# A multi-head attention block on one core: new written-out lists for every engine, and score products with 128-column query weights

## The chip, the core and the metric

The kernel runs on one core of a Trainium2 chip. Five engines each follow a list of their own: TensorE (PE, matrix products; its weight loads are shown as PEld), VectorE (DVE), ScalarE (ACT), GpSimd (POOL) and SyncE (SP), which here only issues DMAs. They wait for one another through semaphores. The metric is the device time of one execution in microseconds (us); lower is better.

## What is computed

```
B, Sq, D = 8, 112, 640          H, Sk, Dh = 32, 512, 192        (all bf16)
q = (x @ wq).reshape(B, Sq, H, Dh).transpose(0, 2, 1, 3)
scores = einsum("bhqd,bhkd->bhqk", q, k_cache) * Dh ** -0.5
p = softmax(scores)
o = einsum("bhqk,bhkd->bhqd", p, v_cache)
out = o.transpose(0, 2, 1, 3).reshape(B, Sq, H * Dh) @ wo
```

The key and value caches are 50 MB each; x, wq, wo and the result are small beside them.

## The kernel before

The 32 heads are taken in four **rounds** of eight. A round goes over the eight batches, and each batch of a round is two **steps** of four heads: 64 steps, numbered n = 0 to 63. Two half-rounds (batches 0 to 3 and 4 to 7) make a **group** g = 0 to 7, which has its own projections and its own output products, each 448 columns wide (4 batches of 112 rows).

What an entry of a list means, with the helper that builds it:

- `XT`, `evX`: x is transposed on TensorE and copied to `xT_sb` (7 pieces).
- `Q(g, lp, c)`, `evQ` (q_fill): five products of 128x448 make a third of the queries of one head pair; ACT copies them to `qr`. 96 entries.
- `KT(i, p)`, `evK` (k_transposes): the keys of the first seven batches are loaded as they are (`KN`), transposed on TensorE and copied to `kt`. From batch 7 on a DMA transposes them on the way (`K`).
- `qc(n)`: DVE copies parts of `qr` to `qh`, moved by 64 partitions, as the 192 dimensions of a head are 128 + 64.
- `Sm(n, j)`, `St(n, ...)` (scores): the score products. Queries are the weights, keys the moving operand. Sm holds eight products per step over all 128 rows of the array; St holds eight over 64 rows each, which run two at a time on the two halves. They always use PSUM banks 0 to 3.
- `smax`, `exp`, `rc`, `norm` (softmax): DVE copies a head's scores to `s_sb` (three buffers) with the row minimum of the negated scores, ACT takes the exponential with its sum, DVE takes the reciprocal and scales. Four heads per step.
- `PT(n)`, `evPT` (transposes): 32 small transposes turn the probabilities; ACT and DVE copy half each to `pT_sb`. For steps 57 to 61 a DMA does it instead (`TD`).
- `PVt`, `PVm`, `evPV` (values): the products with the values, 16 that use half of the array's columns and 16 full ones; ACT copies the result to `oT_sb`.
- `O(g, m, part)`, `oacc`: twelve products per block m of the output, in two halves, added up in `accT`. `O6`, `OL`, `OF`, `oout` and `OUT` do the last batches, the final transposes and the stores.

So TensorE has three shapes on its array: full (XT, Q, Sm, PVm, O, OF), row halves (KT, St, PT) and column halves (PVt).

The order is not left to a planner: `ORDER_PE`, `ORDER_ACT`, `ORDER_DVE` and `ORDER_SP` are lists in the code, and each engine runs its own strictly in order. An entry waits for those named as its dependencies, and for the copies that free its PSUM bank; the bank stands in the entry of ORDER_PE, and `fill` adds the wait. The loads go out on SP's one queue in ORDER_SP's order: a load waits at the head of the queue until its buffer is free (four buffers for keys, three for values, one for wo, four separate pieces for wq). `exp` of step n also waits for PT or TD of step n - 2, whose probabilities lie in the same buffer.

The lines of the profile: L546 XT, L561 KT, L590 Q, L635 and L637 Sm, L648 and L650 St, L706 PT, L739 PVt, L750 PVm, L772 O; L572 evK, L595 evQ, L612 and L613 qc, L663 smax, L668 exp, L672 norm, L680 rc, L719 evPT, L760 evPV, L787 oacc; L139 K, L150 V, L162 X, L171 KN, L183 WQ, L193 WO, L690 TD. L578 are idle products before any data has come.

## Time and profile before

| | |
|---|---|
| time, three runs | 443.73, 445.71 and 450.0 us; median 445.71 |
| span of the profiled execution | 444.4 us (no time around the span is given) |
| PE busy | 425.1 us, 96% of the span, 6805 products |
| weight loads busy | 304.5 us, 69% |
| DVE busy | 363.2 us, 82% |
| ACT busy | 344.4 us, 78% |
| SP | 100 DMAs, 122 MB moved, 275 GB/s |
| granted TensorE clock, mean | 0.996 |

Busy times on PE overlap: a product begins before the one ahead has drained. What a product costs when they follow one another is the distance of two starts, which the timeline gives. In a row of groups, the number after the busy time is the mean duration in ns of one instruction, and behind the bar stands the idle time of the engine just before such instructions with what ended it. In a merged row of the timeline, "x5" says how many instructions it holds, and its length runs from the first start to the last end.

### The profile page before, as it was taken

The numbers are of one execution on the slowest core, as the hardware profiler recorded it, in microseconds if no ns is written. First come the engines' busy times: TensorE is split into PE (matmuls) and PEld (weight loads), VectorE is DVE, ScalarE is ACT, GpSimd is POOL, SyncE is SP. The second block draws the span as 40 slices with busy tenths as digits, with TensorE's granted clock in tenths as the row PEclk, the third lists the DMA queues.
The fourth block names the chain that finished last, engine by engine and source line by source line (L and its number), as shares of the span: only waits on it lengthen the run. The fifth ranks groups of instructions, "written<-read, shape, count | busy, mean of one in ns | idle before, by whom it ended". The sixth has DMA issues, their size and how long they took to land.

```text
span 444.4 us, 16108 instructions
## 1 busy us (share of the span) xinstructions
PE 425.1 (96%) x6805; PEld 304.5 (69%) x6805; DVE 363.2 (82%) x1165; ACT 344.4 (78%) x770; POOL 0.7 (0%) x6
## 2 busy tenths in 40 slices
PE   6998989889999999999899999999999999899995
PEld 4666666666677667777677766767667766676895
DVE  1579999879699889888989798889799888969871
ACT  3699999887678687978869688788778758965773
POOL 0000000000000000000000000000000000000000
PEclk9999999999999999999999999999999999989999
DMA  8999999998999999999999999999999999999952
GB/s 278 373 337 323 347 299 285 226 342 276 232 289 317 215 270 270 365 247 288 238 223 324 301 236 267 360 370 234 234 266 313 256 267 371 234 173 242 237 176 80
DMA packets 222184, 122.02 MB, mean 275 GB/s; under 512 B 164640, under 2 KB 222112, under 8 KB 222112
## 3 DMA queue, kind: packets, MB, share of 16 engines
q1 hardware_dynamic: 222112, 120.99, 106.6%
q8 instruction: 54, 0.88, 0.8%
q14 instruction: 18, 0.15, 0.1%
HBM read 78.22 MB, written 1.15 MB: 179 GB/s over the span
## 4 chain that ended last, share of the span: by engine, by line
PE 84%; DVE 5%; ACT 5%; DMA 4%; issue 2%; SPq 0%; ACTq 0%
PE ps L772 19%; PE ps L590 18%; PE ps L750 12%; PE ps L648 7%; PE ps L739 7%; PE ps L635 6%; PE ps L637 6%; PE ps L706 5%; DVE s_sb L663 3%; DMA wo_sb<-in_k_cache_dram 2%; PE ps L561 2%; ACT p_sb L668 2%; DMA wq_sb<-in_wq_dram 2%; ACT qr L595 1%; DVE p_sb L672 1%
## 5 line engine op out<-in xcount | busy, mean ns | idle before, releaser
L668 ACT ACTIVATE p_sb<-s_sb,nmx 112x512 bf16<-112x512 f32 x256 | 182.8, 717 | 31.6 <-DVE s_sb L663 26.8
L663 DVE TENSOR_SCALAR_CACHE_REDUCE s_sb<-ps 112x512 f32<-112x512 f32 x256 | 169.4, 684 | 29.6 <-PE ps L650 20.8
L590 PE MATMUL ps<-xT_sb,wq_sb 128*128 128x448 bf16 x480 | 102.0, 353 | 3.3 <-DMA wq_sb<-in_wq_dram 2.3
L772 PE MATMUL ps<-oT_sb,wo_sb 128*128 128x448 bf16 (+1 forms) x480 | 93.3, 341 | 0.1
L672 DVE TENSOR_SCALAR p_sb<-p_sb,rinv 112x512 bf16<-112x512 bf16 x256 | 81.3, 347 | 1.5
L590 PEld LDWEIGHTS ps<-xT_sb,wq_sb 128*128 128x128 bf16 x480 | 42.9, 98 | 41.5 <-DMA wq_sb<-in_wq_dram 2.9
L772 PEld LDWEIGHTS ps<-oT_sb,wo_sb 128*128 128x128 bf16 x480 | 44.3, 98 | 35.0 <-DVE pT_sb L719 0.5
L760 ACT ACTIVATE oT_sb<-ps 128x672 bf16<-128x672 f32 x64 | 46.3, 726 | 25.8 <-PE ps L750 25.4
L595 ACT ACTIVATE qr<-ps 128x448 bf16<-128x448 f32 x96 | 49.6, 539 | 12.7 <-PE ps L590 12.1
L750 PE MATMUL ps<-pT_sb,vt 128*128 128x112 bf16 x944 | 55.8, 215 | 2.0 <-issue 2.0
L719 ACT ACTIVATE pT_sb<-ps 128x768 bf16<-128x768 bf16 x59 | 47.0, 801 | 12.8 <-PE ps L706 12.8
L750 PEld LDWEIGHTS ps<-pT_sb,vt 128*128 128x128 bf16 x944 | 48.1, 99 | 6.3 <-issue 2.1
L668 ACT ACTIVATION_READ_ACCUMULATOR p_sb<-s_sb,nmx 112x1 f32 x256 | 49.5, 193 | 0.0
L719 DVE COPY pT_sb<-ps 128x1024 bf16<-128x1024 bf16 x59 | 40.3, 683 | 3.4 <-PE ps L706 2.6
L706 PE MATMUL ps<-ident,p_sb 64*128 64x64 bf16 (+1 forms) x1888 | 37.3, 185 | 1.2 <-issue 0.6
L706 PEld LDWEIGHTS ps<-ident,p_sb 64*128 64x128 bf16 (+1 forms) x1888 | 33.3, 94 | 5.8 <-DVE p_sb L672 2.0
L635 PE MATMUL ps<-kt,qr 128*112 128x256 bf16 x128 | 36.0, 282 | 0.9 <-ACT oT_sb L760 0.4
L637 PE MATMUL ps<-kt,qh 128*112 128x256 bf16 x128 | 35.2, 275 | 1.1 <-issue 1.1
L635 PE MATMUL ps<-kt,qh 128*112 128x256 bf16 x128 | 35.1, 274 | 0.0
L637 PE MATMUL ps<-kt,qr 128*112 128x256 bf16 x128 | 35.0, 274 | 0.0
L650 PE MATMUL ps<-kt,qh 64*112 64x256 bf16 x128 | 34.1, 291 | 0.1
L648 PE MATMUL ps<-kt,qr 64*112 64x256 bf16 x128 | 34.0, 291 | 0.0
(62 smaller groups left out, 478.6 us busy)
## 6 DMA issues: line engine op xcount, KB each, us to landing
vt<-in_v_cache_dram SPq DMA_DIRECT2D x32, 1536.0 KB, 9.0
wo_sb<-in_wo_dram SPq DMA_DIRECT2D x4, 1920.0 KB, 12.7
wq_sb<-in_wq_dram SPq DMA_DIRECT2D x14, 480.0 KB, 5.7
wo_sb<-in_k_cache_dram SPq DMA_DIRECT2D x3, 1536.0 KB, 9.3
accT<-in_k_cache_dram SPq DMA_DIRECT2D x3, 1536.0 KB, 12.7
vt<-in_k_cache_dram SPq DMA_DIRECT2D x2, 768.0 KB, 10.0
out_dram<-xT_sb SPq DMA_DIRECT2D x8, 140.0 KB, 3.2
wq_sb<-in_wq_dram SPq DMA_DIRECT2D x1, 960.0 KB, 10.6
```

Source lines behind the costliest of these rows:

```text
L590: mm = e.matmul(ps[:, bank, 0:SG], wq_sb[:, dc, c0:c0 + 128], xT_sb[:, dc, bh * SG:(bh + 1) * SG], start=(dc == 0), stop=(dc == DC - 1))
L595: return e.activation(qr[:, q_slot(g, lp), c, :], ps[:, bank, 0:SG], ACTF.Copy)
L635: e.matmul(ps[0:SQ, 2 * j, hs], ev, ktb[:, :, 0, cs(i)], start=(h == 0), stop=False, skip_group_check=True)
L637: mm = e.matmul(ps[0:SQ, 2 * j + 1, hs], od, ktb[:, :, 2, cs(i)], start=(h == 0), stop=False, skip_group_check=True)
L648: m1 = e.matmul(ps[0:SQ, 2 * j, hs], ev, ktb[0:64, :, 1, cs(i)], start=False, stop=True, skip_group_check=True)
L663: return e.tensor_scalar(s_sb[:, a, :].rearrange("p (e c) -> p e c", e=2), ps[0:SQ, 2 * j:2 * j + 2, h * 256:(h + 1) * 256], -scale, None, ...
L668: return e.activation(p_sb[:, k, :], s_sb[:, a, :], ACTF.Exp, bias=nmx[:, k:k + 1], scale=-1.0, accum_out=rsum[:, k:k + 1])
L672: return e.tensor_scalar(p_sb[:, k, :], p_sb[:, k, :], rinv[:, k:k + 1], None, op0=ALU.mult)
L706: ends.append(e.transpose(psb[:, bank + t, i * w:(i + 1) * w], p_sb[lo:hi, (4 * n + k) % 8, q * 128:(q + 1) * 128], ident[lo:hi, lo:hi]))
L719: return e.activation(dst, src, ACTF.Copy) if j == 0 else e.tensor_copy(dst, src)
L750: mm = e.matmul(ps[:, b0 + j, 2 * h * SQ:(2 * h + 1) * SQ], vtb[:, h0 + 2 * j + h, d0:d0 + 128], pT(j, h, q), start=(q == 0), stop=(q == 3))
L772: mm = e.matmul(ps[:, bank_of["O", g, m, 0], 0:nc_], wo_sb[:, k, m * 128:(m + 1) * 128], oT_sb[:, g % 2, k, 0:nc_], start=(k == 0), stop=( ...
```

## The change

Three things change; the products keep their number, their rows and their moving operands.

1. **All lists are new**: the order of TensorE, ACT, DVE and of the loads, and the PSUM bank of each tile, which now stands in a list `BANKS` of its own. Which of ACT and DVE copies a tile now follows from the list that holds the copy: ACT has 22 key copies (25 before) and five of x (four), DVE 34 and two. Bank waits are found from the list (`tiles`, `holder`), and each of them names all copies of the bank. St comes as two entries per step instead of four, so other work may stand between Sm and St.
2. **Score products read 128 query columns** as their weights, where they read 112. The buffers `qr` and `qh` become flat, `qr` with 16 columns of padding behind each head pair (`QP = 3 * SG + 16`); the 16 extra columns are the neighbour's queries or zeros and make score rows 112 to 127, which nothing reads. DVE clears the padding at the start, and TensorE waits for that.
3. Some **dependencies are written out**: the reciprocal waits for the normalisations two steps back, a copy of PV or of the transposed probabilities names all three entries of the step.

The core of the diff:

```diff
-        qr = sb("qr", [128, QS, 3, SG], BF16)
-        qh = sb("qh", [128, 2, 2, 4, SQ], BF16)
+        qr = sb("qr", [128, QS * QP], BF16)
+        qh = sb("qh", [128, 2 * 2 * 4 * SQ + 16], BF16)
...
+        def q_at(n, j, c, lo, hi):
+            r, b, qd = place(n)
+            c0 = (q_slot(group(n), 2 * qd) + j) * QP + c * SG + b % (B // 2) * SQ
+            return qr[lo:hi, c0:c0 + 128]
+        def h_at(n, j, k, lo, hi):
+            c0 = ((n % 2 * 2 + j) * 4 + k) * SQ
+            return qh[lo:hi, c0:c0 + 128]
...
-                        e.matmul(ps[0:SQ, 2 * j, hs], ev, ktb[:, :, 0, cs(i)], start=(h == 0), stop=False,
+                return e.matmul(ps[:, 2 * j + odd, hs], q, ktb[lo:hi, :, blk, cs(2 * j + h)],
+                                start=first, stop=last, skip_group_check=True)
...
-                add("DVE", ("rc", n, j), [("exp", n, 2 * j), ("exp", n, 2 * j + 1)], rc)
+                add("DVE", ("rc", n, j), [("exp", n, 2 * j), ("exp", n, 2 * j + 1),
+                                          ("norm", n - 2, 2 * j), ("norm", n - 2, 2 * j + 1)], rc)
...
         ORDER_SP = [
-            ("X", 0), ("X", 1), ("WQ", 0, 1, 1), ("WQ", 0, 0, 1), ("KN", 0, 0, 4), ("X", 2), ("WQ", 0, 2, 2),
+            ('WQ', 0, 1, 1), ('X', 1), ('X', 0), ('WQ', 0, 0, 1), ('X', 2), ('WQ', 0, 2, 2), ('KN', 0, 0, 4),
...
-            ("V", 23), ("V", 25), ("K", 28), ("K", 27), ("K", 29), ("V", 27), ("V", 26), ("WO", 3), ("V", 28),
-            ("K", 30), ("K", 31), ("TD", 57), ("TD", 58), ("V", 29), ("TD", 59), ("V", 30), ("TD", 60), ("TD", 61),
+            ('V', 26), ('K', 29), ('K', 30), ('V', 28), ('V', 27), ('V', 29), ('K', 31), ('TD', 57), ('TD', 58), ('WO', 3),
+            ('TD', 59), ('V', 30), ('TD', 60), ('TD', 61), ('V', 31), ('OUT', 1), ('OUT', 0), ('OUT', 2), ('OUT', 5),
...
+        for op in ORDER_PE:
+            for bank, evacs in tiles(op):
+                P.ops[op]["banks"] = P.ops[op]["banks"] + holder.get(bank, [])
+                holder[bank] = evacs
...
+            e.memset(qr[:].rearrange("p (l w) -> p l w", w=QP)[:, :, 3 * SG:QP], 0.0)
+            e.memset(qh[0:64, 0:16 * SQ].rearrange("p (j k s) -> p j k s", j=4, k=4)[:, :, 0, :], 0.0)
+            e.memset(qh[64:128, 0:16 * SQ].rearrange("p (j k s) -> p j k s", j=4, k=4)[:, :, 3, :], 0.0)
+            e.memset(qh[:, 16 * SQ:], 0.0).then_inc(zINIT, 1)
```

TensorE's new list, near round 3's first output products (ORDER_PE), and DVE's at step 58 (ORDER_DVE):

```
PE:  ... ('St', 59, 1), ('O', 5, 2, 1), ('PVt', 55), ('PVm', 55, 0), ('PVm', 55, 1), ('Sm', 60, 0), ('Sm', 60, 1),
     ('St', 60, 0), ('St', 60, 1), ('PVt', 58), ('PVt', 56), ('PVm', 56, 0), ('PVm', 56, 1), ('PVm', 58, 0), ('PVm', 58, 1),
     ('Sm', 61, 0), ('Sm', 61, 1), ('St', 61, 0), ('St', 61, 1), ('PVt', 57), ('PVm', 57, 0), ('PVm', 57, 1), ('O', 6, 1, 0) ...
DVE: ... ('rc', 58, 0), ('rc', 58, 1), ('norm', 58, 1), ('norm', 58, 3), ('norm', 58, 2), ('oacc', 5, 4), ('norm', 58, 0) ...
```

The code has two more forms that the change does not use: pairs of projections over half the rows (`QPAIRS`, empty) and score products over half the rows alone (`ROWS`, empty).

## The prediction

> **What bounds the kernel now.** First the page: the span, the busy shares, the chain that ended last.

> ```profile
> span 444.4 us, 16108 instructions
> PE 425.1 (96%) x6805; PEld 304.5 (69%) x6805; DVE 363.2 (82%) x1165; ACT 344.4 (78%) x770; POOL 0.7 (0%) x6
> PE 84%; DVE 5%; ACT 5%; DMA 4%; issue 2%; SPq 0%; ACTq 0%
> ```

> TensorE carries 84% of the chain, so the time is its list plus its gaps. The windows say where the gaps are; the columns are us of busy time and instructions of PE, weight loads, DVE, ACT and POOL, then clock, DMA share and GB/s.

> ```profile
> 0.00:40.00 40.00, 36.63 (x530) 23.52 (x530) 21.68 (x63) 27.74 (x57) 0.70 (x6) 1.00 0.95 322
> 40.00:80.00 40.00, 36.04 (x817) 26.93 (x816) 37.76 (x120) 38.12 (x84) 0.00 (x0) 1.00 1.08 315
> 80.00:93.30 13.30, 11.68 (x247) 8.22 (x245) 11.09 (x37) 11.33 (x25) 0.00 (x0) 1.00 1.11 269
> 120.00:160.00 40.00, 40.00 (x586) 28.07 (x585) 35.58 (x113) 30.86 (x71) 0.00 (x0) 1.00 1.19 271
> 280.00:320.00 40.00, 39.95 (x599) 27.52 (x600) 33.52 (x111) 32.94 (x75) 0.00 (x0) 1.00 1.14 302
> 360.00:400.00 40.00, 37.44 (x580) 27.20 (x579) 33.44 (x111) 29.51 (x69) 0.00 (x0) 0.96 1.08 267
> ```

> There are two stages. From 40 to 80 us DVE (37.76 of 40) and ACT (38.12) are full and TensorE waits for them. From 120 us on TensorE is full (40.00) and they have room. A busy PE is not one at its peak, so I take what an instruction costs from the starts of neighbours:

> ```profile
> 153.41 0.27 PE L635 MATMUL ps<-kt,qh 128*112 128x256 bf16 x1
> 153.42 0.13 PEld L637 LDWEIGHTS ps<-kt,qr 128*112 128x112 bf16 x1
> 153.52 0.27 PE L637 MATMUL ps<-kt,qr 128*112 128x256 bf16 x1
> 153.73 0.31 PE L648 MATMUL ps<-kt,qr 64*112 64x256 bf16 x1
> 154.30 0.98 PE L739 MATMUL ps<-pT_sb,vt 128*64 128x112 bf16 x32
> 155.21 1.75 PE L750 MATMUL ps<-pT_sb,vt 128*128 128x112 bf16 x32
> 156.79 1.11 PE L590 MATMUL ps<-xT_sb,wq_sb 128*128 128x448 bf16 x5
> ...
> 378.32 0.27 PE L637 MATMUL ps<-kt,qr 128*112 128x256 bf16 x1
> 378.52 0.31 PE L648 MATMUL ps<-kt,qr 64*112 64x256 bf16 x1
> 378.90 0.27 PE L650 MATMUL ps<-kt,qr 64*112 64x256 bf16 x1
> 379.10 0.74 PE L590 MATMUL ps<-xT_sb,wq_sb 128*128 128x448 bf16 x3
> ```

> A main score product starts 0.11 us after the one before (153.41, 153.52). Where the shape on the array changes, it is 0.20 to 0.21 (153.52 to 153.73), so a change of shape costs 0.095. A projection product takes (1.11 - 0.35)/4 = 0.19, a value product 1.75/32 = 0.05, a narrow one 0.98/32 = 0.03.

> **The change, part by part.** *The 128 columns.* The weight loads, grouped by shape:

> ```profile
> L635 PEld LDWEIGHTS ps<-kt,qr 128*112 128x112 bf16 x128 | 16.7, 130 | 8.6 <-DVE s_sb L663 3.1 <-issue 0.8 <-ACT oT_sb L760 0.5
> L648 PEld LDWEIGHTS ps<-kt,qr 64*112 64x112 bf16 x128 | 16.0, 125 | 11.4 <-issue 11.4
> L590 PEld LDWEIGHTS ps<-xT_sb,wq_sb 128*128 128x128 bf16 x480 | 42.9, 98 | 41.5 <-DMA wq_sb<-in_wq_dram 2.9 <-ACT kt L572 1.0 <-issue 0.6
> ```

> A load of 112 columns takes 125 to 130 ns, one of 128 takes 98. Eight groups of 128 make 1024 score loads; 1024 x 32 ns is 33 us of busy time that goes. But each load lies beside the product before it (load at 153.42, its product at 153.52, products 0.11 apart without a gap), so that cover hides it. The change of shape does not show it either: 378.32 to 378.52 waits for a load of 112 columns and 378.90 to 379.10 for one of 128, and both are 0.20. What can still be open is the first load after a wait, at most one per step and 64 x 32 ns = 2 us. Bounds: 0 to 2 us gained, and below that 33 us if all were exposed, which the rows exclude. I take 0. [...]

> *TensorE's list.* It holds the same 736 entries. Counted in the two lists, changes of shape between neighbours fall from 254 to 246: 8 x 0.095 = 0.8 us off.

> *The first loads.* The query weights' first piece now goes ahead of the two pieces of x.

> ```profile
> 0.74 0.97 SPq L162 DMA_DIRECT2D kt<-in_x_dram  x2
> 4.41 1.28 PE L546 MATMUL ps<-ident,kt 128*128 128x128 bf16 x20
> 7.66 1.12 PE L590 MATMUL ps<-xT_sb,wq_sb 128*128 128x448 bf16 x5 [1.97 <-DMA wq_sb<-in_wq_dram]
> 9.08 0.74 PE L590 MATMUL ps<-xT_sb,wq_sb 128*128 128x448 bf16 x3 [0.29 <-DMA wq_sb<-in_wq_dram]
> 19.09 0.69 DVE L663 TENSOR_SCALAR_CACHE_REDUCE s_sb<-ps 112x512 f32<-112x512 f32 x1 [1.66 <-PE ps L650]
> ```

> The same bytes are there at about 7.6 us, but the transposes of x (1.28 us in all) and their copies, hidden under the wait until now, then stand behind them: the first projection starts near 9.0 instead of 7.66, 1.4 later; the wait at 9.08 (0.3) goes. Net +1.0 (0.5 to 2.3). The extra memsets at the start lie before 4.41 and cost nothing.

> *The first ten steps.* Here DVE and ACT set the pace. Up to the last normalisation of step 9 DVE's list has 33 key evacuations instead of 30, one more row minimum (smax), one query copy (qc) and one copy of x fewer. From the rows

> ```profile
> L663 DVE TENSOR_SCALAR_CACHE_REDUCE s_sb<-ps 112x512 f32<-112x512 f32 x256 | 169.4, 684 | 29.6 <-PE ps L650 20.8 <-PE ps L648 4.2 <-ACT p_sb L668 3.5
> L572 DVE COPY kt<-ps 128x768 bf16<-128x768 bf16 x31 | 16.5, 551 | 10.5 <-PE ps L561 10.5
> L612 DVE COPY qh<-qr 64x672 bf16<-64x672 bf16 x64 | 21.1, 329 | 4.0 <-PE ps L650 1.2 <-ACT qr L595 0.9
> 92.41 0.88 DVE L672 TENSOR_SCALAR p_sb<-p_sb,rinv 112x512 bf16<-112x512 bf16 x3
> 95.68 0.63 PE L706 MATMUL ps<-ident,p_sb 64*128 64x64 bf16 x32
> ```

> that is 3 x 0.55 + 0.68 - 0.66 - 0.5, or 1.2 us more of busy time and, as neighbours overlap by some 0.08, about 0.9 more of pace. In the trace that normalisation ends at 92.41 + 0.88 = 93.3 and step 9's transposes start at 95.68. TensorE's list ahead of them, by the spacings above (34 projection entries of five x 0.19, 11 steps of scores at 1.30, 28 key entries at about 0.31, nine transposes at 0.44, eight value steps at 1.22, x 2.0, 57 changes of shape at 0.095), is 76.3 us, so TensorE had stood 19.4 us by then. In the new list it is 72.1 (29 projections, 12 steps of scores, 27 key entries, 52 changes of shape): scores come earlier, projections later. With the same DVE gaps step 9's transposes follow at 93.3 + 0.9 = 94.2, and TensorE has stood 22.1: 2.7 worse. DVE's gaps are 40 - 21.68 = 18.3 before 40 us, and 2.2 + 2.2 from there to 93.3; by busy time these 4.4, by pace some 7, would vanish at best: 87.3, and TensorE has stood 15.2: 4.2 better. TensorE's larger lead argues for fewer DVE gaps; I take the middle, -1, the later start included.

> *The middle.* From 120 us TensorE was full. The work between a step's last score product and its own transposes, which hides the softmax chain, falls at the median over the steps from 12.2 to 11.7 us; its least value up to step 56 falls from 9.4 to 8.8. The room behind a transpose before its banks are wanted again falls from 3.4 to 2.9, behind a value product from 1.9 to 1.5. That costs 0 if the chains still fit, 5 us if each of some ten tight places loses half a microsecond. I take +1. Against it stand waits for nothing in the list:

> ```profile
> PE ps L750 <- issue: 2.0, 1, 2.0
> PE ps L561 <- issue: 2.0, 2, 1.1
> PE ps L637 <- issue: 1.1, 1, 1.1
> ```

> These 5 us may recur elsewhere or go; I leave them in.

> *The loads.* The same hundred DMAs stand in one queue in another order; a key transpose holds the queue some 6.8 us when others follow. The output weights of round 3 now stand behind the transposing DMAs of steps 57 and 58.

> ```profile
> 386.93 6.83 SPq L139 DMA_TRANSPOSE kt<-in_k_cache_dram  x1
> 398.29 4.36 SPq L690 DMA_TRANSPOSE wq_sb<-p_sb  x2
> wo_sb<-in_wo_dram SPq DMA_DIRECT2D x4, 1920.0 KB, 12.7
> DMA to landing us min/median/max: 7.1/12.0/14.7
> ```

> They may start once O(5,2,1) is done and step 58's normalisation, which now waits behind oacc(5,4) on DVE, has let its DMA be issued. From O(5,2,1) to the first use, O(6,1,0), the new list has 8.2 us of TensorE's work (four narrow entries, eight value entries, two steps of scores, eight changes of shape); the old one had 22.9. The load takes 12.7 at the median, beside other loads; 7.1, the least of a 1536 KB load into the same tile, scaled to 1920 KB, is an estimated 8.9. About 0.7 goes to the issue of step 58's DMA. Bounds: 8.9 + 0.7 - 8.2 = 1.4 to 14.7 + 0.7 - 8.2 = 7.2. No other load is released beside it, so near the lower end: +2. Behind TensorE's wait stand the score products of steps 62 and 63, the last ones. The same transposing DMA feeds step 58's values, 10.6 us of list behind its scores; that fits within half a microsecond and is taken as 0. The reciprocal's new wait names normalisations of DVE's own list two steps back, long done: 0. The other loads keep the lead that they had or more than a landing, but KN(4): 8.1 us instead of 20.5, bounds 0 to 2, taken as 0.

> **The sum.** 444.4 - 0.8 - 1 + 1 + 2 = 445.6 in the profiled execution's own terms (its span; no time around it is given). The three runs have median 445.71, 1.3 above that span; so 446.9, rounded to **446.5**.

> **The rivals.** *DVE becomes the bound for longer, slower.* In steps 9 to 12 DVE's list lies within some 3 us of TensorE's in the new order, 8 to 11 us before. An item that comes late on DVE's strict list then stops TensorE at once. DVE's list up to step 11's last normalisation is 79.5 us by pace, TensorE's ahead of that step's transposes 82.3. If DVE has gaps of 30 us by then (93.3 less 68.1 us of list is 25 at step 9 in this trace), TensorE stands 79.5 + 30 - 82.3 = 27 us, not some 20: +7. With the sum's +1 and +2 it is 444.4 - 0.8 + 7 + 1 + 2 = 453.6, or 455 as a median, +2.1%; from those 30 us it decides. For it: the full window of 40 to 80. Against it: DVE waited mostly for TensorE (20.8 us behind L650 in the row above), which now brings scores earlier. 18%.

> *The late output weights alone.* 7.2 instead of 2 gives 452: +1.4%. 12%.

> *The early gaps go.* -4.2 instead of -1, the 5 us of issue waits gone, +1 for the loads: 444.4 - 0.8 - 4.2 - 5 + 1 = 435.4, about 436.7, -2.0%. Against it: start and evacuations leave no more. 18%, half of it beyond 2%.

> *The loads set the score products' pace.* If each of the 512 main products had to wait for its load, 512 x 32 ns = 16 us would go: 430. The rows speak against it: 0.11 apart with loads of 0.13 beside. 3%. [...]

> **How the numbers follow.** The forecast has 49%, the rivals 18, 12, 18 and 3. Faster by over 2% (about what a measurement of this kernel can tell from no change): 9 + 3 = 12%. Slower: the first rival's 18%. Within: 49 + 12 + 9 = 70%. The range leaves out the fall by the loads and most of the slow tail: 437 to 456.

> **What would show it.** Score loads at 98 ns with products still 0.11 apart: the columns are worth nothing. First projection near 9.0. Step 9's transposes between 87 and 94 us. TensorE full from 120 us. A wait of TensorE for wo_sb of 1 to 7 us after 395 us. The prediction is wrong if products stand closer than 0.11, if TensorE still has gaps past 120 us for DVE or ACT, or if step 9 comes after 97.

## The result, and the profile after

The changed kernel takes 461.04 us at the median of four runs (459.41 to 465.59), the kernel before 445.25 beside it: 1.0352 times as long, 95% interval 1.0265 to 1.0438. That is slower, and outside the range. The profiled execution is the longest of the four, 465.59, so its parts add up to some 4.5 us more than the median.

First the page of the changed kernel: span, busy shares, the chain that ended last.

```profile
span 463.8 us, 16105 instructions
PE 432.8 (93%) x6805; PEld 291.7 (63%) x6805; DVE 365.4 (79%) x1171; ACT 343.3 (74%) x768; POOL 0.7 (0%) x6
PE 67%; DVE 13%; DMA 11%; issue 4%; ACT 3%; SPq 0%; DVEq 0%; ACTq 0%
```

TensorE's share of the chain has fallen from 84% to 67%; DVE and DMA have taken it. So the list of TensorE no longer sets the time alone. The windows say where (columns: busy time of PE, weight loads, DVE, ACT, POOL, then clock, DMA share, GB/s). First three of the kernel before that are not shown above, then the changed kernel:

```profile
93.30:120.00 26.70, 25.46 (x405) 17.84 (x403) 20.05 (x63) 18.51 (x43) 0.00 (x0) 1.00 1.01 268
320.00:360.00 40.00, 39.77 (x592) 27.84 (x590) 35.53 (x114) 31.50 (x71) 0.00 (x0) 1.00 1.17 266
400.00:444.00 44.00, 39.55 (x630) 33.05 (x627) 29.16 (x97) 26.80 (x58) 0.00 (x0) 1.00 0.73 185
```

```profile
40.00:80.00 40.00, 32.87 (x724) 23.18 (x725) 34.63 (x110) 32.98 (x72) 0.00 (x0) 0.98 1.00 271
80.00:93.30 13.30, 12.45 (x263) 8.32 (x262) 10.49 (x33) 10.68 (x22) 0.00 (x0) 0.93 1.06 375
93.30:120.00 26.70, 22.89 (x406) 15.82 (x404) 20.92 (x69) 20.75 (x48) 0.00 (x0) 0.94 0.93 204
120.00:160.00 40.00, 39.66 (x618) 26.24 (x610) 34.65 (x114) 31.21 (x71) 0.00 (x0) 1.00 1.17 250
320.00:360.00 40.00, 36.31 (x468) 22.72 (x466) 28.35 (x94) 26.89 (x63) 0.00 (x0) 0.91 1.15 291
400.00:440.00 40.00, 37.19 (x437) 24.41 (x438) 32.51 (x110) 23.08 (x58) 0.00 (x0) 0.96 0.99 211
```

Three places lose: 40 to 120 us, 320 to 360, 400 to 440. In each the granted clock is below 1 too (0.93 to 0.98, then 0.91, then 0.96). What TensorE waited for (sum, times, longest, in us):

```profile
PE ps L911 <- DMA wo_sb<-in_wo_dram: 4.8, 2, 2.7
PE ps L877 <- issue: 3.4, 2, 3.2
PE ps L744 <- issue: 3.4, 1, 3.4
PE ps L688 <- DMA wq_sb<-in_wq_dram: 1.5, 2, 0.9
PE ps L877 <- DMA vt<-in_v_cache_dram: 1.2, 2, 0.7
PE ps L744 <- DMA kt<-in_k_cache_dram: 0.9, 1, 0.9
```

Before, no load of this table held TensorE after 50 us. Now four kinds do, and the waits for nothing ("issue") reach 3.4 us each. The timeline shows what stands behind such a gap (L688 Q, L744 scores, L845 PT, L877 and L889 the values, L911 O):

```profile
8.96 2.61 PE L688 MATMUL ps<-xT_sb,wq_sb 128*128 128x448 bf16 x10 [0.68 <-DVE xT_sb L134]
...
78.48 0.37 PE L744 MATMUL ps<-kt,qh 64*128 64x256 bf16 x1 [3.40 <-issue]
...
78.81 3.52 PE L688 MATMUL ps<-xT_sb,wq_sb 128*128 128x448 bf16 x10
...
97.51 0.64 PE L845 MATMUL ps<-ident,p_sb 64*128 64x64 bf16 x31
...
109.16 0.68 PE L877 MATMUL ps<-pT_sb,vt 128*64 128x112 bf16 x9 [3.18 <-issue]
...
335.36 2.40 PE L911 MATMUL ps<-oT_sb,wo_sb 128*128 128x448 bf16 x6 [2.69 <-DMA wo_sb<-in_wo_dram]
...
422.17 5.06 PE L911 MATMUL ps<-oT_sb,wo_sb 128*128 128x448 bf16 x17 [2.10 <-DMA wo_sb<-in_wo_dram]
```

Ten projection products behind the gap at 78.48 take 3.52 us, 0.35 apart on average instead of 0.19. The granted clock of this trace is 0.50 from 78.4 us on for 3.4 us, and likewise at the other three gaps of over 2 us: from 109.1 for 3.4, from 334.4 for 6.8, from 423.1 for 3.4. That is 17.1 us at half the clock, which the table below prices at 7.9, beside 11.4 us for the four gaps themselves.

And the load queue (SPq; the middle number is how long the loads held it until the last was issued):

```profile
251.18 29.43 SPq L142 DMA_TRANSPOSE kt<-in_k_cache_dram  x3
...
293.50 27.21 SPq L142 DMA_TRANSPOSE kt<-in_k_cache_dram  x3
320.77 0.57 SPq L153 DMA_DIRECT2D vt<-in_v_cache_dram  x1
321.39 0.58 SPq L196 DMA_DIRECT2D wo_sb<-in_wo_dram  x1
```

The output weights of round 2 (L196) could have gone at 314.2, when the last output product of round 1 was done. They went at 321.39, behind three key transposes, landed at 335.2, and TensorE stood.

To compare runs I add up TensorE's standing time from the starts of neighbouring products: what a start lies later than the usual spacing of its kind (0.19 for a projection, 0.11 for a score product and so on, and 0.095 for a change of shape), from 0.06 us on, by the releaser that the trace names. Without a releaser I count up to 0.195 us too late as the half clock, more as a wait for nothing. In us, each from one profiled execution:

| | span | DVE | ACT | loads | nothing | half clock |
|---|---|---|---|---|---|---|
| before | 444.4 | 3.3 | 4.4 | 4.1 | 6.7 | 1.6 |
| changed | 463.8 | 10.5 | 2.2 | 9.3 | 11.0 | 7.9 |
| e1 old lists | 443.4 | 4.3 | 4.2 | 3.5 | 7.5 | 3.1 |
| e2 112 columns | 458.4 | 11.1 | 2.0 | 5.6 | 11.0 | 3.4 |
| e5 without K7, K8 | 453.4 | 9.6 | 2.7 | 6.7 | 7.1 | 5.7 |
| e9 new lists, few loads | 444.1 | 11.2 | 2.8 | 1.7 | 5.0 | 2.8 |
| e10 old lists, few loads | 436.5 | 4.9 | 4.1 | 5.3 | 0.5 | 0.9 |
| e12 other order at 300 us | 460.5 | 10.5 | 2.1 | 7.6 | 13.3 | 4.1 |
| e14 as e9, short minima | 436.7 | 2.9 | 4.0 | 2.4 | 4.7 | 2.3 |
| e15 as e10, short minima | 432.2 | 1.1 | 5.1 | 4.0 | 1.0 | 0.7 |
| e16 old lists, K7 later | 450.4 | 4.6 | 4.4 | 12.2 | 5.2 | 1.7 |

### The profile page after: what moved, and what is told of

Read it like the earlier page. It is cut to its first block, busy times and chain, and to the rows that moved or that the text cites. A ratio compares the mean times of both kernels' runs of the same rounds, so it can differ in the third digit from the quotient of the medians.

```text
span 463.8 us, 16105 instructions
## 1 busy us (share of the span) xinstructions
PE 432.8 (93%) x6805; PEld 291.7 (63%) x6805; DVE 365.4 (79%) x1171; ACT 343.3 (74%) x768; POOL 0.7 (0%) x6
## 4 chain that ended last, share of the span: by engine, by line
PE 67%; DVE 13%; DMA 11%; issue 4%; ACT 3%; SPq 0%; DVEq 0%; ACTq 0%
PE ps L688 17%; PE ps L744 15%; PE ps L911 14%; PE ps L889 8%; DVE s_sb L801 6%; PE ps L845 5%; DMA wo_sb<-in_wo_dram 5%; PE ps L877 5%; DMA wq_sb<-in_wq_dram 5%; DVE p_sb L810 2%; ACT p_sb L806 2%; PE ps L640 1%; DVE qh L729 1%; DVE qh L730 1%; DMA kt<-in_x_dram 1%
## 5 line engine op out<-in xcount | busy, mean ns | idle before, releaser
L688 PE MATMUL ps<-xT_sb,wq_sb 128*128 128x448 bf16 x480 | 102.9, 360 | 3.6 <-DMA wq_sb<-in_wq_dram 1.5
L744 PE MATMUL ps<-kt,qr 128*128 128x256 bf16 (+1 forms) x512 | 98.2, 275 | 2.9 <-DVE s_sb L801 1.2
L911 PE MATMUL ps<-oT_sb,wo_sb 128*128 128x448 bf16 (+1 forms) x480 | 96.2, 348 | 4.8 <-DMA wo_sb<-in_wo_dram 4.8
L744 PE MATMUL ps<-kt,qh 128*128 128x256 bf16 (+1 forms) x512 | 89.1, 274 | 3.4 <-issue 3.4
L688 PEld LDWEIGHTS ps<-xT_sb,wq_sb 128*128 128x128 bf16 x480 | 43.9, 99 | 46.3 <-issue 6.9
L911 PEld LDWEIGHTS ps<-oT_sb,wo_sb 128*128 128x128 bf16 x480 | 44.6, 99 | 40.6 <-issue 6.0
L744 PEld LDWEIGHTS ps<-kt,qr 128*128 128x128 bf16 (+1 forms) x512 | 44.3, 96 | 29.4 <-issue 15.3
L889 PE MATMUL ps<-pT_sb,vt 128*128 128x112 bf16 x944 | 56.4, 215 | 0.0
L889 PEld LDWEIGHTS ps<-pT_sb,vt 128*128 128x128 bf16 x944 | 48.6, 99 | 5.3 <-issue 0.4
L744 PEld LDWEIGHTS ps<-kt,qh 128*128 128x128 bf16 (+1 forms) x512 | 44.6, 97 | 5.1 <-issue 0.2
L845 PE MATMUL ps<-ident,p_sb 64*128 64x64 bf16 (+1 forms) x1888 | 38.0, 186 | 3.2 <-issue 1.2
L845 PEld LDWEIGHTS ps<-ident,p_sb 64*128 64x128 bf16 (+1 forms) x1888 | 33.4, 94 | 10.5 <-DVE p_sb L810 3.0
L877 PE MATMUL ps<-pT_sb,vt 128*64 128x112 bf16 x944 | 33.9, 216 | 6.2 <-issue 3.4
L877 PEld LDWEIGHTS ps<-pT_sb,vt 128*64 128x64 bf16 x944 | 25.9, 110 | 20.4 <-issue 7.1
## 6 DMA issues: line engine op xcount, KB each, us to landing
wo_sb<-in_wo_dram SPq DMA_DIRECT2D x4, 1920.0 KB, 12.4
vt<-in_k_cache_dram SPq DMA_DIRECT2D x2, 768.0 KB, 10.6
```

The lines of the kernel that those rows point to most:

```text
L688: mm = e.matmul(ps[:, bank, 0:SG], w, v, start=(dc == 0), stop=(dc == DC - 1))
L744: return e.matmul(ps[:, 2 * j + odd, hs], q, ktb[lo:hi, :, blk, cs(2 * j + h)], start=first, stop=last, skip_group_check=True)
L845: ends.append(e.transpose(psb[:, bank + t, i * w:(i + 1) * w], p_sb[lo:hi, (4 * n + k) % 8, q * 128:(q + 1) * 128], ident[lo:hi, lo:hi]))
L877: mm = e.matmul(ps[64 * h:64 * h + 64, b0 + j, SQ:2 * SQ], vtb[:, h0 + 2 * j + h, d0:d0 + 64], pT(j, h, q), start=(q == 0), stop=(q == 3))
L889: mm = e.matmul(ps[:, b0 + j, 2 * h * SQ:(2 * h + 1) * SQ], vtb[:, h0 + 2 * j + h, d0:d0 + 128], pT(j, h, q), start=(q == 0), stop=(q == 3))
L911: mm = e.matmul(ps[:, bank_of["O", g, m], 0:nc_], wo_sb[:, k, m * 128:(m + 1) * 128], oT_sb[:, g % 2, k, 0:nc_], start=(k == 0), stop=(k = ...
```

## The experiments

Two theories at the start: the order of the loads costs most of the time; or the order of the engines' lists does, with DVE too late. All kernels have the 128 columns unless said. Ratios are to the kernel before on the same chip. In the edits K24 stands for the entry ("K", 24), and so on.

### Lists or columns (e1, e2)

```diff
 e1: ORDER_PE, ORDER_ACT, ORDER_DVE, ORDER_SP, BANKS = those of before
 e2: -   return qr[lo:hi, c0:c0 + 128]     (and qh; ps[:, ...] likewise)
     +   return qr[lo:hi, c0:c0 + SQ]
```

> The lists of the engines, the list of the loads and the banks are those of the kernel before; the 128 columns, the cleared padding and the written-out waits of the new code stay. Theory (the lists, above all that of the loads, cost the time): as the kernel before, 444 to 448 us, ratio 0.995 to 1.005. Rival (the columns or the new code's waits cost it): 455 to 461 us, ratio at least 1.02.

> New lists and loads, but each score product reads 112 query columns, as before. Theory (columns are worth nothing): as the changed kernel, 458 to 463 us. Rival (the wider weights cost): 445 to 450. A third view (the wider weights gain and the lists lose more): above 465. In the trace, score loads at 125 to 130 ns again and products still 0.11 us apart.

e1: 444.47 us, ratio 0.9971 (0.9935 to 1.0006). e2: 460.25, ratio 1.0338 (1.0299 to 1.0378). The groups of weight loads of the main score products, first of the changed kernel, then of e2:

```profile
L744 PEld LDWEIGHTS ps<-kt,qr 128*128 128x128 bf16 x256 | 25.2, 98 | 14.0 <-DVE s_sb L801 5.8 <-DVE rinv L818 1.3 <-issue 0.8
```

```profile
L744 PEld LDWEIGHTS ps<-kt,qr 128*112 128x112 bf16 x256 | 32.5, 131 | 11.5 <-DVE s_sb L801 5.6 <-DVE qh L730 0.6 <-DVE rinv L818 0.6
```

The weight loads of the changed kernel are 33 ns shorter and the time is the same. The lists cost everything, the columns nothing.

### Loads or engines (e3, e9, e10)

```diff
 e3:      ORDER_SP without ("V", 3) to ("V", 31)
 e9, e10: ORDER_SP without these and without ("K", 7) to ("K", 31); e10 with the lists of e1
```

> New lists, but the value loads from the fourth batch on are left out, so that the products with values read old values and the output is not the reference's; 29 of 100 DMAs and some 43 of 122 MB go. Theory (the queue of loads falls behind): TensorE's waits for loads past 120 us (9 us) go, with them the slow clock behind the longest of them, and, if the waits for nothing come from the traffic of the loads, most of their 12 us: 443 to 450 us. Rival (DVE's and TensorE's lists are out of step, whatever the loads do): 455 us or more.

> New lists without the 25 transposing key loads and the 29 value loads from the fourth batch on; later steps read old keys and values, and the output is not the reference's. What is left on the queue are x, the projection weights, the first keys and values and the output weights. Theory (some three quarters of the loss come from the queue of loads, by waits for loads, late fetches of instructions and the slow clock behind them; the rest from waits of TensorE for DVE that the new order has more of): 442 to 446 us, 3 to 7 above the next run. Rival (with the loads gone both are alike): within 2 us of the next run. Second rival (the order of the engines' lists carries most): 10 us or more above the next run.

> The same loads left out, with the lists and banks of before in the new code; the output is not the reference's. Theory (the kernel before has only its late fetches to lose, 5 to 7 us of waits for nothing): 437 to 441 us. Rival (its waits for nothing have another cause than loads): 443 to 445, as with all loads.

e3: 448.80, ratio 1.0073 (1.0041 to 1.0106). e9: 445.81, 1.0035 (1.0014 to 1.0055). e10: 437.10, 0.9828 (0.9793 to 0.9864). The chains that ended last, of e9 and then of e10:

```profile
PE 68%; DVE 18%; ACT 6%; issue 4%; DMA 3%; SPq 0%; DVEq 0%; ACTq 0%
```

```profile
PE 84%; DVE 5%; ACT 5%; DMA 4%; issue 1%; SPq 0%; DVEq 0%; ACTq 0%
```

With all loads the new lists lose 461.04 - 444.47 = 16.6 us to the old ones; with few loads 8.7. So neither theory holds alone: about half of the loss is there only while the loads run, half without them. I had given the loads three quarters. In e10 the waits for nothing are all but gone (7.5 to 0.5 us): with the old lists they belong to the loads.

### What the loads do (e5, e4, e12, e6, e11, e16)

```diff
 e5:  ORDER_SP without ("K", 7) and ("K", 8)
 e4:  +  twelve products ps[:, bank of O(4,0), 0:448] = ident x xT_sb ahead of O(4,0,0), ten ahead of O(6,1,0)
 e12: -  K24, K25, K23, V22, WO2, V23
      +  K23, K24, V22, WO2, K25, V23
 e6:  from WO0 to K31 a new order, by the time of first use: e.g. K9 ahead of K10, WO2 and V23 ahead of K25
```

> New lists, but the first two transposing key loads (batches 7 and 8) are left out, so that their steps read old keys and the output is not the reference's. In the changed kernel a fetch of instructions that usually comes every 7 to 8 us comes 12 us after the one before while the load of batch 7 is being issued, and TensorE stands 3.6 us there and 3.3 us at a second place, with products half as fast behind. Theory (the fetches are late because the transposing loads are under way, and the rest of the queue is ahead by what these two take): both waits for nothing go and the slow products behind them, 6 to 10 us, and some of the later waits for loads: 448 to 455 us. Rival (the waits for nothing belong to the place in the list, whatever the loads do): they stay, at 2.5 us or more each, and the time with them, 457 to 462.

> New lists; twelve products of 448 columns whose result nothing reads stand ahead of TensorE's wait for the output weights of round 2, and ten ahead of that for round 3, in the banks that the output products then overwrite. They take 2.3 and 1.9 us of waits of 2.9 and 2.3. Theory (a gap of over two us is followed by some 4 us at half clock, which costs as much again as the wait): the waits stay, the products behind them stand 0.19 apart instead of 0.37, 4 us less than the changed kernel, 455 to 458 us. Rival (the slow products are slow for another reason, such as the loads that are under way): no change, 460 to 462, and 0.37 apart as before.

> New lists; in the loads keys 23 go ahead of keys 24, and the output weights of round 2 ahead of keys 25. Nothing else moves. Theory (the wait of 2.9 us for these weights, the 1.1 us for keys 23 and the half clock behind come from two transposing loads that stand ahead of them): they go, 3 to 6 us less than the changed kernel, 455 to 458 us. Rival (the queue is full, the wait moves to the next load): 459 to 462.

> New lists of the engines and banks; only the order of the loads differs, from the output weights of round 0 on: set by when each is wanted, with the output weights of round 2 some 9 us earlier in the queue, keys 23 ahead of keys 24 and 25, keys 20 ahead of 21. The first 25 loads stay. Theory (the order of the loads costs TensorE its waits past 120 us, 3 to 9 us with the slow clock): these waits go but that for the output weights of round 3, and 452 to 456 us are left, above the kernel before because of DVE and the waits for nothing in the first 120 us. Rival (the queue is full, whatever its order): the waits move to other loads, 458 to 462.

e5: 454.51, ratio 1.0214 (1.0143 to 1.0285), 6.5 us less than the changed kernel. Where TensorE had stood 3.40 us, its timeline has this left:

```profile
76.50 0.27 PE L744 MATMUL ps<-kt,qh 64*128 64x256 bf16 x1 [0.38 <-issue]
```

The wait at 109 us is gone too. So without these two loads one long wait for nothing shrinks and the other goes. What stands behind them the trace shows in part. The page of the changed kernel lists a queue of instructions beside that of the loads:

```profile
q8 instruction: 53, 0.87, 0.8%
```

These are 53 packets of 16 KB, and TensorE has 13610 products and weight loads: 257 to a packet, and a packet every 8.75 us on average (463.8 / 53). That the packets are TensorE's I take from this count and from e13. In the changed kernel and the kernel before, all ten waits for nothing of over 0.35 us on TensorE end 1.2 to 1.6 us after one of these packets has landed. In the changed kernel packets come at 63.9 and then at 75.8 us, when the load of keys 7 has been issued (67.4 to 75.8); for 64.2 to 75.6 us its view of the queues lists only

```profile
q1 hardware_dynamic: 6357, 2.59, 112.7%
```

and no line for q8. But in e9, which has neither of these loads, two packets lie as far apart (62.8 and 74.7 us), and TensorE stands 1.67 us behind them. So the long interval alone does not show that the load held the packet up; how the load lengthens the wait stays open.

e4: 459.56, ratio 1.0336 (1.0291 to 1.0380). In its profiled execution the stretches behind the two waits run at full clock:

```profile
320.00:360.00 40.00, 39.90 (x562) 26.03 (x559) 32.83 (x108) 29.43 (x68) 0.00 (x0) 1.00 1.15 285
400.00:440.00 40.00, 38.47 (x539) 27.04 (x537) 29.32 (x93) 22.34 (x51) 0.00 (x0) 1.00 0.84 195
```

The clock went from 0.91 and 0.96 to 1.00. That filling the gaps did this is not shown: in e2 TensorE stands 2.22 and 2.15 us for the same two loads, nothing fills these gaps, and the clock is 1.00 in both windows all the same. Nor does the profiled execution stand for the others: its mean clock is 0.995, theirs 0.984 to 0.987, as low as the changed kernel's (0.982 to 0.991). The median is only 1.5 us lower, within the spread of four runs (456.62 to 461.94): as a saving it is unclear.

e12: 462.60, ratio 1.0397 (1.0351 to 1.0443). The waits at 322 and 332 us are gone, and in its timeline this one stands in their place:

```profile
395.57 0.96 PE L877 MATMUL ps<-pT_sb,vt 128*64 128x112 bf16 x16 [5.22 <-DMA vt<-in_v_cache_dram]
```

Values 27 land at 395.4, 1.5 us earlier than in the changed kernel's profile, but TensorE gets there 10 us earlier, at 390. What was gained in front is given back to the queue, and my theory of one misplaced pair of loads fell. e6 reordered the whole queue: ratio 1.0343 (1.0239 to 1.0446). From its profile (span 464.0 us) I read where TensorE waits, not how much the order costs. No wait for a value, key or projection load is left past 120 us, but its list of waits has new ones:

```profile
PE ps L744 <- DVE s_sb L801: 6.1, 4, 3.8
PE ps L845 <- issue: 5.1, 2, 4.1
PE ps L889 <- issue: 2.7, 1, 2.7
```

The first of these is a load in disguise. Most of it stands at step 60: its score products wait for the row minima of step 59, those for a score buffer, that for an exponential of step 59, and that for the transposing DMA of step 57, which stood behind keys 31 and landed at 412.2. The waits for nothing have come at new places, 99 and 136 us. The rival was right for both kernels: the queue is full. An estimate from rows above and of before: 25 transposes at 6.8 us and the other 83 MB at 375 GB/s (the highest rate in the windows above, at 80 us) are some 390 us, and in the changed kernel the issue of a transpose behind plain loads ended 3.3 to 5.1 us after they had landed (last section).

If so, a small edit should cost the old lists too. Two edits in the loads of e1:

```diff
 e11: -  K29, V27, V26, WO3, V28, K30, K31
      +  K29, K30, V26, V27, WO3, V28, K31
 e16: e11, and
      -  V4, K7, K8, WO0, V6, V5, V7
      +  V4, WO0, V5, K7, K8, V6, V7
```

> The lists of before in the new code, with one edit in the loads: keys 30 go out right behind keys 29, ahead of values 26 and 27, the output weights of round 3 and values 28, and hold the queue some 7 us instead of 15. Theory (the late fetch at 387 us, 2 to 2.7 us, comes because keys 30 hold the queue for 15 us): that wait goes or shrinks under 1 us, 441 to 443.5 us, ratio to the kernel before 0.990 to 0.997. Rival (the fetch is late wherever a transposing load is under way): the wait moves, 444 to 446.

> The lists of before in the new code with the edit of keys 30 of e11, and keys 7 and 8 sent out behind the output weights of round 0 and values 5, some 12 us later. Theory (between 80 and 104 us three late fetches of 1 us each come with these two loads, which are wanted only 29 and 39 us after they land): one or two of them go, 440 to 442.5 us, ratio to the kernel before 0.988 to 0.995. Rival (they come late with any load that is under way): 442.5 to 444, as e11.

e11: 443.04, ratio 0.9959 (0.9934 to 0.9984). In e1 keys 30 go out at 372.13, behind the output weights and values 28, and TensorE then stands at 387 for 2.50 us, with slow products behind. I put this down to a late packet: in the kernel before, the wait of 1.96 us at this place ends 1.4 us after a packet that came 11.7 us behind the last (375.2, 386.9). First e1's queue, then its timeline:

```profile
372.13 22.42 SPq L142 DMA_TRANSPOSE kt<-in_k_cache_dram  x2
```

```profile
389.74 0.27 PE L892 MATMUL ps<-pT_sb,vt 128*128 128x112 bf16 x2 [2.50 <-issue]
```

In e11 that wait is gone. Keys 31 now hold the queue 16.6 us behind plain loads (from 379.75 us), and yet packets come at 385.0 and 393.1 and TensorE does not stand: here a load held the queue for long and no packet was late. e11 is the fastest version found that does the whole work, by 0.4% against the kernel before; that it is faster than e1 is not shown (their intervals overlap). e16: 453.61, ratio 1.0217 (1.0179 to 1.0254), 10.6 us more than e11, with the engines' lists of before. Its queue around the edit, and its waits:

```profile
80.86 21.68 SPq L142 DMA_TRANSPOSE kt<-in_k_cache_dram  x2
```

```profile
PE ps L880 <- DMA vt<-in_v_cache_dram: 4.8, 2, 3.3
PE ps L691 <- DMA wq_sb<-in_wq_dram: 4.2, 4, 2.0
PE ps L914 <- DMA wo_sb<-in_wo_dram: 1.5, 1, 1.5
```

These waits stand at 192 and at 248 to 294 us. Keys 7 and 8 went out 11 and 15 us later than in e1, were still early, and yet the delay was handed on for 200 us, which fits a queue with little room to catch up (the 390 us above). My expectation missed by 11 us. The order of the loads alone can cost two thirds of what the whole change costs (10.6 of 15.8 us).

### What is left without loads (e7, e8, e14, e15, e13)

```diff
 e7, e8:   - norm: p_sb[:, k, :] = p_sb[:, k, :] * rinv
           + norm: p_sb[:, k, 0:256] = p_sb[:, k, 0:256] * rinv        (e8 with the lists of e1)
 e14, e15: - smax reads ps[0:SQ, 2 * j:2 * j + 2, h * 256:(h + 1) * 256]
           + smax reads ps[0:SQ, 2 * j:2 * j + 2, h * 256:h * 256 + 128]   (on e9 and e10)
 e13:      + 64, 128, 256, 512 transposes of ident ahead of PT 20, 30, 40, 50 (on e10)
```

> New lists; each normalisation scales only 256 of its 512 columns, so half of the probabilities stay unscaled and the output is not the reference's. That takes some 30 us of work off DVE (256 times about 0.13 us). Theory (in the new lists DVE is late in its strict list, 11 us of TensorE's waits against 3 to 4 before): these waits fall to some 3 us, 450 to 455 us. Rival (the waits lie in the order of the lists, DVE waits for TensorE and ACT as often): less than 2 us less than the changed kernel, 459 to 461.

> The same halved normalisation, with the lists, loads and banks of before in the new code; the output is not the reference's. Theory (with the old lists DVE holds TensorE for only 4 us): 1 to 4 us less than with the full normalisation, 440 to 443 us. Rival (DVE paces both alike): 8 us less or more, 436 or below.

> New lists without the later loads, as in e9, and each row minimum reads 256 of its 512 scores, so that it takes about 0.4 us instead of 0.68 (the other half of the copied scores stays zero; the output is not the reference's). Theory (the row minima free the score banks too late for the new order): TensorE's waits for DVE fall from 11 to 5 us or less, 438 to 441 us against 445.8. Rival (the waits stand for other things, such as the exponentials that free the three score buffers, or the normalisations): 443 to 446.

> The same halved row minima with the lists of before and without the later loads, as in e10. Theory: the old order has 5 us of waits for DVE, and 1 to 3 go: 434 to 436 us against 437.1; the distance to e14 is 3 to 6 us instead of 8.7. Rival: the distance stays near 9.

> The lists of before in the new code without the later key and value loads, as in e10, and four bursts of small products whose result nothing reads: 64, 128, 256 and 512 transposes of 64 rows ahead of the transposes of steps 20, 30, 40 and 50. A product and its weight load are two instructions, so a burst of 512 is 1024 instructions, 64 KB, where TensorE's instructions come in packets of 16 KB. Theory (instructions come no faster than one packet in some 4 us): the bursts of 64 and 128 run at 14 ns a product; those of 256 and 512 stop one to three times for 1 to 3 us, and the last takes 12 to 17 us. Rival (packets keep up when no loads are under way): all run at 14 ns, 0.9, 1.8, 3.6 and 7.2 us.

e7: 460.20, ratio 1.036 (1.028 to 1.0439); e8: 444.62, 0.9992 (0.9952 to 1.0031). DVE lost 15 us of busy time (350.2 against 365.4; I had expected 30) and nothing came of it: TensorE still waits 10.9 us for DVE. So this work, taken off DVE, does not help. e14: 438.72, 0.9884 (0.9838 to 0.9929); e15: 433.48, 0.9758 (0.9707 to 0.9809). The group of the row minima of e14, and its chain that ended last:

```profile
L796 DVE TENSOR_SCALAR_CACHE_REDUCE s_sb<-ps 112x256 f32<-112x256 f32 x256 | 102.2, 418 | 50.8 <-PE ps L739 28.8 <-ACT p_sb L801 16.4 <-PE ps L872 1.6
```

```profile
PE 88%; ACT 5%; DMA 3%; issue 2%; DVE 1%; SPq 0%; ACTq 0%; DVEq 0%
```

With 418 ns instead of 684 the waits for DVE fall from 11.2 to 2.9 us, DVE's share of the chain from 18% to 1%, and the distance between new and old lists from 8.7 to 5.2 us. So what the new order seems to lack is room between a score product and whatever wants its bank, or its step's probabilities, next: the chain from product to row minimum is too long for it. That it is the length of the chain and not DVE's load is argued from e7, not shown: e14 also takes 60 us of work off DVE (304.7 us busy against 364.9 in e9), four times as much as e7. Of the last 5.2 us the table gives 3.7 to waits for nothing, 1.6 to the half clock and 1.8 to waits for DVE; waits for loads and ACT are 2.7 less. e13 (456.32 us, ratio 1.0276) measures the rate of the packets; the burst of 512 in its timeline:

```profile
357.52 3.03 PE L856 MATMUL ps<-ident 64*128 64x64 bf16 x196
361.77 2.04 PE L856 MATMUL ps<-ident 64*128 64x64 bf16 x128 [1.23 <-issue]
365.50 2.04 PE L856 MATMUL ps<-ident 64*128 64x64 bf16 x128 [1.69 <-issue]
369.23 1.05 PE L856 MATMUL ps<-ident 64*128 64x64 bf16 x60 [1.69 <-issue]
```

The bursts of 64, 128 and 256 ran through at 14.5 ns a product (0.91, 1.84 and 3.71 us); the theory had the 256 stop. That of 512 stopped after 196 products and then every 128, which with their weight loads are 256 instructions, about the 257 of a packet: one per 3.73 us, with hardly a load under way. Each time TensorE ran through them in 2.04 us and stood 1.69 us. That this is what happens at the four places of e9 (30, 47, 56 and 75 us) is argued from the rate; it was not tried by moving them.

## Why the prediction was wrong, point by point

- *The 128 columns*: right. Loads at 98 ns, products 0.11 apart, nothing gained (e1, e2).
- *Shape changes, -0.8*: counted in the lists; too small to be measured here.
- *The first loads, +1.0*: right, the first projection starts at 8.96 and waits for the copy of x.
- *The first ten steps, -1*: wrong. Step 9's transposes come at 97.51, past the 94.2 and past 97, the limit that I had set; by then TensorE has stood 25.4 us (97.5 less 72.1 of list), not 15.2 to 22.1. Of these, 6.0 lie before its first product, 6.8 are waits for nothing, the half clock behind them adds some 2, and some 5 are waits for DVE, where the kernel before has 1.3 up to the same place. I had set these ten steps by DVE's work alone. With few loads (e9) step 9's transposes come at 94.45, near the 94.2.
- *The middle, +1*: the right way, but too small. From 120 to 360 us the waits for DVE rise from 0.8 to 2.2 us, behind that from 1.2 to 2.5. So the two terms for DVE, -1 and +1, add up to nothing, while TensorE's waits for DVE rise by 7.2 us in the whole (3.3 to 10.5), and by 6.3 with few loads (e10 to e9).
- *Waits for nothing, "I leave them in"*: wrong. 11.0 us instead of 6.7. They end 1.2 to 1.6 us after a packet of instructions has landed (changed kernel and before), are longer with loads (11.0 us against 7.1 in e5, 7.5 in e1 against 0.5 in e10), and move with both orders.
- *The late output weights, +2*: the wait was right, 2.10 to 2.27 us at 420, in its bounds of 1.4 to 7.2. The half clock behind it, some 2 us more, was not in the term.
- *"The other loads keep the lead that they had or more than a landing"*: this step failed, and the term for it was nothing. I compared, for each load, the work of TensorE between release and use with a landing time. That counts the queue as empty. It holds each load behind the transposes ahead of it: the output weights of round 2 waited 7 us for their turn. What runs only with the loads is 7.9 of the 16.6 us (e1, e9, e10), waits for nothing and half clock included. The other 8.7 are there without them, and there it is the terms for DVE that failed.
- *Rival, DVE becomes the bound for longer, 455*: the nearest, and its condition was all but met. Step 11's last normalisation ends at 109.2, 29.7 us behind DVE's list of 79.5 (its mark was 30), and step 9's transposes start 0.06 us behind that step's last normalisation (97.45, 97.51), where they had 2.4 us of room (93.3, 95.68). Less work for DVE did not help in e7; shorter row minima win back 3.5 us of the loss (e14, e15). That its 455 comes near 461 is in part luck: of the loads it counts only the +2 for the late output weights.
- *Rival, the early gaps go, 436.7*: the opposite came, waits for nothing rose. *Rival, late output weights alone, 452*: the wait stayed at the low end. *Rival, loads set the score products' pace*: refuted by e2 (loads of 131 ns instead of 98, 460.25 us against 461.04).
- *The sum* comes to 446.9; the 446.5 of the forecast is not its rounding. Nothing hangs on the difference.

Open: how the 5.2 us that are left in e14 against e15 divide up at the level of single entries, what makes a packet late, and what decides whether the clock falls at a gap.

## What to carry to other kernels

Judge a new order of loads on one queue by the queue: go through it load by load with its release, the time that it holds the queue and its landing, and see where the first one is late. Here a queue that was busy nearly all the time passed a delay on for some 200 us (e16). Where a list packs many small products together, count instructions as well as time (in e13 TensorE stood 1.69 us after every 256). And try to shorten the chain that frees a bank first: here that paid (e14, 7.1 us less than e9), and taking other work off the engine that ends the chain did not (e7).
